# Attention scores as 64-row products, one PSUM bank per head, with q copied once and the second element's means moved

## The chip, the cores and the metric

The kernel runs on one core of a Trainium2 chip. A core has five engines that run their own instruction streams: TensorE (PE: matrix products and, as PEld, the loading of the stationary operand), VectorE (DVE), ScalarE (ACT), GpSimd (POOL) and SyncE (SP), which here issues all transfers between memory and the on-chip buffers. Products land in PSUM, which is used here as eight banks of 128 partitions by 512 float32. The metric is the device time of one execution in microseconds; the time of a kernel is the median of its runs.

## The reference

Attention over 4 elements of a batch, 8 heads, 768 positions and 64 values per head, then a two-layer network over the 3,072 rows. Each position sees its neighbours within 15 positions and a summary of each of the 24 blocks of 32 positions: the maximum of the block's keys and the mean of its values.

```python
block, window = (32, 16)
nb = S // block
scale = 1.0 / np.sqrt(D)
k_sum = k.reshape(B, H, nb, block, D).max(axis=3)
v_sum = v.reshape(B, H, nb, block, D).mean(axis=3)
scores_l = scale * np.matmul(q, k.transpose(0, 1, 3, 2))
mask_l = np.abs(pos[:, None] - pos[None, :]) < window
scores_s = scale * np.einsum('bhsd,bhnd->bhsn', q, k_sum)
scores_s = scores_s + np.log(block)
scores_l_m = np.where(mask_l, scores_l, -1000000000.0)
scores_all = np.concatenate([scores_l_m, scores_s], axis=-1)
...
a = np.exp(scores_all)
a = a / (np.sum(a, axis=-1, keepdims=True) + 1e-09)
v_all = np.concatenate([v, v_sum], axis=2)
return np.matmul(a, v_all).astype(np.float32)
```

```python
h = x @ w_in
g = h - np.tanh(h)
return (g @ w_out).astype(np.float32)
```

`w_in` is 512 x 2048 and `w_out` 2048 x 512. They arrive as 8-byte floats and are turned into float32 on the chip. All arithmetic has float32 accuracy.

## The kernel before

**Units.** Each element is cut into two halves of 384 positions, so there are eight units `u` (`NU`), each of three tiles `i` of 128 positions (`NT`). Heads go in four pairs `p` per unit, so there are 32 pairs (u, p); two pairs share a group `g` of four heads, for which q, k and v are loaded together (`load_qk`, `load_v`).

**One pair.** `prep` transposes q and k of a pair on PE, two heads on top of each other: head `a` = 0 on partitions 0 to 63, head 1 on 64 to 127. The k side is copied whole into `kf`. The q side is copied into `qf` of shape 128 x 2 x 384: head 0 into `[0:64, 0]`, head 1 into `[64:128, 1]`, two copies of 64 partitions ("q high"); the other two quarters were filled with zeros at the start by `zeros`, on POOL. `prep_sums` puts the block maxima into `kf` between the tiles ("top put"). `score` then makes, for each tile, head and half tile of 64 positions, one product of 118 columns: the 128 rows of `qf[:, a]` against 118 columns of `kf`, in which the zeros remove the other head. A pair has twelve such products. They land in two banks: tiles 0 and 1 in the first, tile 2 in the second (`score_of`), the half tiles on output partitions 0 to 63 and 64 to 127. `softmax` takes the minimum with the mask from the bank (DVE, "min"), the exponential (ACT, "exp"), the sum, its inverse and the normalising product; `transpose_probs` turns the probabilities on PE ("p turn"), into the score banks and bank `pX`, and copies them out ("p out"). `value` makes twelve products of 64 columns per pair, and one entry of the plan (`scores_and_values`) issues the values of one pair directly ahead of the scores of the next.

**Block summaries.** For elements 0 and 1 they are made in the head of the kernel. `load_part` loads one piece of k or v (192 KB); `top_pair` makes the maxima of a pair's keys (two "top pre" on DVE, three transposes on PE, a "top max" on DVE), `sum_pair` the means of a pair's values with twelve small products against `blk`, and `place_v` turns the means of two pairs ("mean turn") into `mean`, from where a transfer puts them into `vw` (`put_mean`). `TOPS` and `SUMS` name the slot at which each (element, pair) has its turn; the loads take buffers of the rings `gt`, `gu`, `gv`, `gh`, `gl`, which the network needs only later. In the kernel before, the pieces for element 0 and element 1 both lie in slots 0 to 15. Elements 2 and 3 are handled later in another way (`sum_chunks`, `finish_k`, `finish_v`).

**The network.** `convert` loads one block of weights (512 KB) at a time, 32 in all, and turns it into float32 in four steps on DVE and ACT. Unit 0 uses whole float32 weights (`wf`): for each of 16 blocks `f` an input product ("in", four products of 384 columns, eight instructions, in one of two banks `pH`), the activation on ACT, POOL or DVE, and three output products ("out", 512 columns, in banks `pY0` to `pY2`). For later units the weights are split into two parts of reduced precision, and each product becomes three that run faster. From unit 2 on, half of the input products are replaced by a scheme with seven products for eight, whose operands are stored to and read back from a scratch tensor `scr`.

**The order of the work.** The main loop runs over slots `j`; unit 0 and its attention fill slots 0 to 15, and the network of unit `u` follows its attention by `LAG` = 22 slots. Each piece of work is an entry of a plan with its reads, writes and a cost. `Plan.schedule` places them on the engines by priority, which is the length of the path behind an entry plus the tables `BIAS` and `KB`; `SL` says when an entry may go to its second engine. The instructions are then issued in that order and stay in it. In the first 100 us, gaps on PE are filled with products of `ident` by itself (`keep_warm`), which nobody reads. Every operation is recorded through one helper, so the profile shows line L72 for all of them, and tiles tell them apart: `q` is `qf`, `k` is `kf`, `pS`, `pX`, `pY` and `pH` are banks, `th` holds the maxima.

The second half of `attention_moe_kernel` repeats the program without the shortcut for small activations; it is behind a test and does not run with these inputs.

Of the kernel before, what the change touches and what calls it, by code (L numbers as in the profile page):

```python
# [15 lines left out]
ALU = mybir.AluOpType  # L16
# [8 lines left out]

PLAIN = 3
# [11 lines left out]

PREP = [0, 2, 6, 11]

TOPS = {0: [(0, 0)], 1: [(0, 2)], 3: [(0, 1)], 5: [(0, 3)], 9: [(1, 3)], 11: [(1, 2)], 13: [(1, 0)], 15: [(1, 1)]}
SUMS = {0: [(0, 0)], 1: [(0, 1), (1, 1)], 8: [(0, 2)], 9: [(0, 3)], 10: [(1, 0)], 11: [(1, 2)], 13: [(1, 3)]}

SIGNED = set()
# [60 lines left out]
class Plan:  # L105
# [56 lines left out]
    def schedule(self, idle):  # L162
# [49 lines left out]
        while total:  # L212
# [88 lines left out]
def program(  # L301
# [129 lines left out]
    ident, mask, blk, ga, small = (made[n,] for n in ("ident", "mask", "blk", "ga", "small"))  # L431
# [21 lines left out]
    def make_blk():  # L453

        gpsimd.memset(blk, 1.0 / 32)
        gpsimd.affine_select(blk, blk, [[1, 3], [-32, NBH]], ALU.is_ge, 0.0, base=0, channel_multiplier=3)
        gpsimd.affine_select(blk, blk, [[-1, 3], [32, NBH]], ALU.is_ge, 0.0, base=31, channel_multiplier=-3)
# [4 lines left out]
    do("const", POOL, 0.7, make_blk, w=[BLK])  # L462
# [14 lines left out]
    for j in range(2):  # L477
        buf(("qf", j), f"q{j}", [P, 2, U])
        buf(("kf", j), f"k{j}", [P, KC])
# [5 lines left out]
    rawq, rawk, vw = (made[n,] for n in ("rawq", "rawk", "vw"))  # L485
    RAWQ = [(("rawq",), i) for i in range(NT)]
    RAWK = [(("rawk",), i) for i in range(4)]

    def vw_keys(i, half):
        return [(("vw",), (i, half, n)) for n in range(3)]  # L490

# [5 lines left out]
    for j in range(2):  # L497
        zeros(j)
# [839 lines left out]
```

## Time and profile before

| | us |
|---|---|
| runs | 730.04, 727.91, 725.0 |
| median | 727.91 |
| profiled execution | 722.92 |
| its span, first to last instruction | 721.2 |

The profile is that of one execution, and its times are counted from its first instruction. A row of instructions has the start, the duration, the engine, the line, the operation with output and inputs, and how many of them were merged; the bracket behind it says how long the engine had been idle and for what. In a row of the chain of waits only the start, the length and the work stand. The merged busy time of PE counts pipelined products, so the distance between starts, or the chain, says what a group really takes.

### The profile page before, as it was taken

Reading aid. Unit: us, or ns where it says so; the run is one execution under the profiler, and the core shown is the slowest. Engines: PE = TensorE matmul, PEld = TensorE weight load, DVE = VectorE, ACT = ScalarE, POOL = GpSimd, SP = SyncE. Lnnn points to the kernel's source line nnn. Section 1 sums busy time; section 2 is a strip of 40 time slices with the busy share of each in tenths; the row PEclk is TensorE's granted clock in tenths of the full one; section 3 lists DMA queues with packets and bytes.
Section 4 is the critical chain, followed back from the end, with each engine's and each line's share of the span. In section 5 each row is a group of like instructions: output and inputs, shape, how many; then the busy total and the mean of one; then the engine's idle time right before and its main releaser. Section 6 shows DMA issues by size and latency. Waiting matters only on the chain.

```text
span 721.2 us, 14213 instructions
## 1 busy us (share of the span) xinstructions
PE 688.8 (96%) x4787; PEld 572.6 (79%) x4787; DVE 431.6 (60%) x1180; ACT 482.3 (67%) x1411; POOL 256.4 (36%) x394
## 2 busy tenths in 40 slices
PE   6898799999999998999999999999999999999995
PEld 5685455558888787889988878998998888999884
DVE  4567878986996645654766557554568533444241
ACT  3467577767789776775897577555669965334981
POOL 3011421131246617422457563433345531111440
PEclk9999899999999999999999999999999999999998
DMA  9989968965665677567465557566544323444101
GB/s 211 234 239 239 307 197 225 281 200 151 202 171 166 179 238 206 138 196 190 123 182 170 164 136 225 142 180 177 170 146 147 119 87 115 147 162 145 45 1 50
DMA packets 158002, 122.67 MB, mean 170 GB/s; under 512 B 94816, under 2 KB 123744, under 8 KB 157920
## 3 DMA queue, kind: packets, MB, share of 16 engines
q1 hardware_dynamic: 157920, 121.67, 58.4%
q8 instruction: 40, 0.66, 0.4%
q14 instruction: 42, 0.34, 0.1%
HBM read 96.21 MB, written 23.07 MB: 165 GB/s over the span
## 4 chain that ended last, share of the span: by engine, by line
PE 77%; DMA 9%; ACT 5%; DVE 3%; SPq 3%; POOL 2%; issue 1%; POOLq 0%; ACTq 0%; DVEq 0%
PE pY L72 34%; PE pH L72 31%; PE pS L72 7%; PE pX L72 5%; SPq L72 3%; DMA wraw<-in_moe_w_in_dram 2%; DMA wraw<-scr 1%; POOL gh L72 1%; ACT prob L72 1%; ACT gu L72 1%; DMA wraw<-in_moe_w_out_dram 1%; DMA gh<-in_v_dram 1%; ACT tmp L72 1%; DVE wf L72 1%; DVE tmp L72 1%
## 5 line engine op out<-in xcount | busy, mean ns | idle before, releaser
L72 PE MATMUL pY<-wf,gh 128*128 128x512 f32 x432 | 178.9, 443 | 5.2 <-POOL gh L72 5.2
L72 PE MATMUL pH<-wh,wraw 128*128 128x384 f32 x672 | 175.3, 342 | 1.3 <-DMA wraw<-scr 1.3
L72 PE MATMUL pY<-wh,gh 128*128 128x512 f32 x336 | 139.4, 415 | 0.0
L72 PE MATMUL pY<-wh,gl 128*128 128x512 f32 x336 | 132.8, 395 | 0.0
L72 PEld LDWEIGHTS pH<-wh,wraw 128*128 128x128 f32 x672 | 120.2, 188 | 9.6 <-DMA wraw<-scr 1.5
L72 POOL TENSOR_TENSOR gu<-gu,gt 128x384 f32<-128x384 f32 x59 | 61.4, 1041 | 185.8 <-ACT gu L72 161.5
L72 ACT ACTIVATE prob<-prob,stat 128x118 f32<-128x118 f32 x248 | 92.3, 384 | 21.3 <-DVE stat L72 20.9
L72 PEld LDWEIGHTS pY<-wf,gh 128*128 128x128 f32 x432 | 80.6, 190 | 30.4 <-issue 12.7
L72 PE MATMUL pH<-wf,wraw 128*128 128x384 f32 x309 | 104.1, 337 | 0.0
L72 PEld LDWEIGHTS pY<-wh,gl 128*128 128x128 f32 x336 | 63.2, 188 | 14.8
L72 PEld LDWEIGHTS pY<-wh,gh 128*128 128x128 f32 x336 | 63.4, 189 | 12.1 <-issue 2.3
L72 ACT ACTIVATE gu<-gu 128x384 f32<-128x384 f32 x128 | 66.9, 523 | 2.2
L72 PE MATMUL pH<-o,wf 128*128 128x384 f32 x188 | 65.3, 446 | 1.6 <-DVE wf L72 1.6
L72 PEld LDWEIGHTS pH<-wf,wraw 128*128 128x128 f32 x309 | 58.0, 188 | 0.0
L72 ACT ACTIVATE gh<-gu 128x384 fp32r<-128x384 f32 x67 | 34.8, 522 | 30.9 <-PE pY L72 21.6
L72 DVE COPY gv<-pH 128x384 f32<-128x384 f32 x50 | 27.9, 558 | 42.4 <-PE pH L72 42.4
L72 DVE CUSTOM_DVE_ANT_0 prob<-pS,mask 128x118 f32<-128x118 f32 x180 | 40.7, 273 | 20.7 <-PE pS L72 20.6
L72 PEld LDWEIGHTS pH<-o,wf 128*128 128x128 f32 x188 | 35.7, 193 | 20.5 <-issue 4.4
L72 ACT ACTIVATE gt<-gu 128x384 f32<-128x384 f32 x42 | 21.9, 523 | 37.1 <-DVE gu L72 36.9
L72 DVE TENSOR_TENSOR gl<-gu,gh 128x384 fp32r<-128x384 f32 x38 | 22.7, 596 | 39.6 <-ACT gh L72 35.7
L72 POOL TENSOR_TENSOR gl<-gu,gh 128x384 fp32r<-128x384 f32 x32 | 33.6, 1055 | 29.4 <-ACT gh L72 27.7
L72 POOL TENSOR_TENSOR gh<-gu,gt 128x384 f32<-128x384 f32 x15 | 23.3, 1555 | 57.3 <-ACT gu L72 33.9
(212 smaller groups left out, 1298.2 us busy)
## 6 DMA issues: line engine op xcount, KB each, us to landing
wraw<-scr SPq DMA_DIRECT2D x75, 512.0 KB
wraw<-in_moe_w_in_dram SPq DMA_DIRECT2D x16, 512.0 KB
wraw<-in_moe_w_out_dram SPq DMA_DIRECT2D x16, 512.0 KB
scr<-wraw SPq DMA_DIRECT2D x16, 512.0 KB
rawq<-in_q_dram SPq DMA_DIRECT2D x48, 128.0 KB
out_dram<-tmp SPq DMA_DIRECT2D x24, 256.0 KB
wraw<-scr SPq DMA_DIRECT2D x21, 256.0 KB
rawk<-in_k_dram SPq DMA_DIRECT2D x32, 128.0 KB
```

The costliest lines, as they stand in the source:

```text
L72: return lambda *args, **kwargs: self._tc.keep_in_program_order(op(*args, **kwargs))
```

## The change

The scores: `qf` loses its second half for one of two buffers (128 x 1 x 384; the other keeps its size because later tiles share it), and the zeros are gone. One copy of 128 partitions replaces two of 64. Each score product takes only the 64 rows of its head, from both `qf` and `kf`, and head `a` lands in bank `a` with its three tiles side by side. The order of the products is now tile, half tile, head.

The means: the pieces of element 1 leave `TOPS` and `SUMS`. Its loads are issued in slots 16 (pairs 0 and 1) and 26 (pairs 2 and 3), eight each time, into the buffers `wh22` to `wh29`; sums and maxima follow in slots 22, 23, 28, 29 and 24, 25, 30, 31, in the banks `pH`. A piece of v is now one head with all its positions, six consecutive positions to a partition, in runs of 1,536 bytes where it was a pair's half in runs of 768 bytes. `sum_pair` has twelve products of 24 columns, all six of a head one after the other, where it had twelve of 12 columns with the heads alternating; `blk` has six planes of 24 columns and lies in the buffer `wh30`.

The plan: `BIAS`, `SL` and `KB` have other numbers throughout, some costs are other numbers, and the products of `keep_warm` are planned with a gap of 0.1 us. The functions `in_runs` and `by_runs` and the branches that use them are not taken, since `RUNS` is 0.

```diff
+RUNS = 0
...
-TOPS = {0: [(0, 0)], 1: [(0, 2)], 3: [(0, 1)], 5: [(0, 3)], 9: [(1, 3)], 11: [(1, 2)], 13: [(1, 0)], 15: [(1, 1)]}
-SUMS = {0: [(0, 0)], 1: [(0, 1), (1, 1)], 8: [(0, 2)], 9: [(0, 3)], 10: [(1, 0)], 11: [(1, 2)], 13: [(1, 3)]}
+TOPS = {0: [(0, 0)], 1: [(0, 2)], 3: [(0, 1)], 5: [(0, 3)]}
+SUMS = {0: [(0, 0)], 1: [(0, 1)], 8: [(0, 2)], 9: [(0, 3)]}
...
-                    d.out = free[PE] = clock.run(free[PE], cost)
+                    d.out = clock.run(free[PE], cost)
+                    free[PE] = d.out + 0.1
...
-    fixed(("blk",), [P, 3, NBH])
+    buf(("blk",), f"wh{2 * NF - 2}", [P, 6, NB])
...
-        buf(("qf", j), f"q{j}", [P, 2, U])
+        buf(("qf", j), f"q{j}", [P, 2 if j else 1, U])
...
-    def zeros(j):
-        for a in range(2):
-            o = 64 * (1 - a)
-            do("const", POOL, 0.75, lambda a=a, o=o: gpsimd.memset(at(("qf", j))[o:o + 64, a], 0.0), w=[(("qf", j), "zero%d" % a)])
...
-                sync.dma_start(st.rearrange("r (a t d) -> r a t d", a=2, t=3), v[b, hs, ts].rearrange("a (r t) d -> r a t d", t=3))
+                sync.dma_start(st, v[b, 2 * p + h].rearrange("(r t) d -> r (t d)", t=6))
...
-            for h in range(2):
-                st = at(("v", b, p, h)).rearrange("r (a t d) -> r a t d", a=2, t=3)
-                for t in range(3):
-                    for a in range(2):
-                        tensor.matmul(at(ps)[D * a:D * (a + 1), NBH * h:NBH * (h + 1)], st[:, a, t], blk[:, t], start=t == 0, stop=t == 2)
+            for a in range(2):
+                st = at(("v", b, p, a)).rearrange("r (t d) -> r t d", t=6)
+                for t in range(6):
+                    tensor.matmul(at(ps)[D * a:D * (a + 1), :NB], st[:, t], at(("blk",))[:, t], start=t == 0, stop=t == 5)
...
-        for a in range(2):
-            rows = slice(64 * a, 64 * a + 64)
-            either("q high", {ACT: 0.42, DVE: 0.5}, lambda e, a=a, rows=rows: copy(e, at(qf)[rows, a], at(pq)[rows, :U], -1.0 / math.sqrt(D)), r=[(pq, 0)], w=[(qf, a)])
+
+        either("q high", {ACT: 0.42, DVE: 0.5}, lambda e: copy(e, at(qf)[:, 0], at(pq)[:, :U], -1.0 / math.sqrt(D)), r=[(pq, 0)], w=[(qf, 0)])
...
-    def score_of(u, p, i):
-        return ("s", u, p, i // 2), 2 * N2 * (i % 2)
+    def score_of(u, p, i, a):
+        return ("s", u, p, a), N2 * i
...
-            s, c = score_of(u, p, i)
-            for a in range(2):
-                for half in range(2):
+            for half in range(2):
+                for a in range(2):
+                    s, c = score_of(u, p, i, a)
                     k0 = KS * i + 64 + 64 * half
-                    tensor.matmul(at(s)[64 * half:64 * half + 64, c + N2 * a:c + N2 * (a + 1)], at(qf)[:, a, P * i + 64 * half:P * i + 64 * half + 64], at(kf)[:, k0:k0 + N2], start=True, stop=True)
+                    rows = slice(64 * a, 64 * a + 64)
+                    tensor.matmul(at(s)[64 * half:64 * half + 64, c:c + N2], at(qf)[rows, 0, P * i + 64 * half:P * i + 64 * half + 64], at(kf)[rows, k0:k0 + N2], start=True, stop=True)
...
-        if B > 1 and j in (23, 31):
-            place_v(1, (j - 23) // 8, "pS1")
+        if B > 1 and j in (16, 26):
+            for n, (kind, p1, h) in enumerate((kind, p1, h) for kind in "vk" for p1 in range(2) for h in range(2)):
+                load_part(kind, 1, p1 + (j - 16) // 5, h, f"wh{22 + n}")
+        if B > 1 and 22 <= j < 32 and (j - 22) % 6 < 4:
+            g, n = divmod(j - 22, 6)
+            if n < 2:
+                sum_pair(1, PG * g + n, "pH")
+                if n == 1:
+                    place_v(1, g, "pS1")
+            else:
+                top_pair(1, PG * g + n - 2, "pH")
```

More of the change, by code (lines that the diff above doesn't have):

```diff
@@ L430, in program @@
     fixed(("small",), [P, 1])
-    ident, mask, blk, ga, small = (made[n,] for n in ("ident", "mask", "blk", "ga", "small"))
+    ident, mask, ga, small = (made[n,] for n in ("ident", "mask", "ga", "small"))
     def make_ident():
@@ L487, in program, with in_runs, by_runs @@
     RAWK = [(("rawk",), i) for i in range(4)]
+    def in_runs(u):
+        return u < RUNS
+    def by_runs(x, n):
+        return x.rearrange("p i h d -> p (i h d)").rearrange("p (h t d) -> p h t d", h=HG, t=n)
     def vw_keys(i, half):
         return [(("vw",), (i, half, n)) for n in range(3)]
-    def zeros(j):
-        for a in range(2):
-            o = 64 * (1 - a)
-            do("const", POOL, 0.75, lambda a=a, o=o: gpsimd.memset(at(("qf", j))[o:o + 64, a], 0.0), w=[(("qf", j), "zero%d" % a)])
-    for j in range(2):
-        zeros(j)
-    do("const", DVE, 0.2, lambda: vector.memset(rawk[0:79, 0], 0.0), w=[RAWK[0]])
-    do("const", DVE, 0.2, lambda: vector.memset(rawk[96:P, 3], 0.0), w=[RAWK[3]])
+    do("const", DVE, 0.3, lambda: vector.memset(rawk[0:79, 0], 0.0), w=[RAWK[0]])
+    do("const", DVE, 0.3, lambda: vector.memset(rawk[96:P, 3], 0.0), w=[RAWK[3]])
     do("const", DVE, 0.2, lambda: vector.memset(vw[0:WIN, 0, 0], 0.0), w=[vw_keys(0, 0)[0]])
@@ L657, in top_pair @@
                    r=[(st[a], 0)] if a else (), w=[(st[0], 0)])
-        do("top turn", PE, 0.325, lambda: [tensor.transpose(at(ps)[:, P * c:P * (c + 1)], at(st[0])[:, P * c:P * (c + 1)], ident) for c in range(3)],
+        do("top turn", PE, 0.42, lambda: [tensor.transpose(at(ps)[:, P * c:P * (c + 1)], at(st[0])[:, P * c:P * (c + 1)], ident) for c in range(3)],
            r=[(st[0], 0), IDENT], w=[(ps, 0)])
@@ L686, in go @@
                 tensor.matmul(at(ps)[:NB, P * pr:P * (pr + 1)], at(x)[:, pr], ident, start=True, stop=True)
-        do("mean turn", PE, 0.5, go, r=[(x, pr) for pr in range(PG)] + [IDENT], w=[(ps, 0)])
+        do("mean turn", PE, 0.55, go, r=[(x, pr) for pr in range(PG)] + [IDENT], w=[(ps, 0)])
         do("mean out", ACT, 0.28, lambda: scalar.activation(mean[32 * g:32 * g + NB], at(ps)[:NB, :HG * D], AF.Copy), r=[(ps, 0)], w=[MEAN[g]])
@@ L798, in transposes @@
         def transposes(ps, raw, n):
+            if in_runs(u):
+                for t in range(n):
+                    for a in (1, 0):
+                        c = ((hs.start + a) * n + t - a) * D
+                        tensor.transpose(at(ps)[:D * (a + 1), :P * n].rearrange("p (r t) -> p t r", t=n)[:, t], raw.rearrange("p i h d -> p (i h d)")[:, c:c + D * (a + 1)], ident)
+                return
             for i in range(n):
                 tensor.transpose(at(ps)[:, P * i:P * (i + 1)], raw[:, i, hs].rearrange("p a d -> p (a d)"), ident)
-        do("q turn", PE, 0.285, lambda: transposes(pq, rawq, NT), r=[*RAWQ, IDENT], w=[(pq, 0)])
-        do("k turn", PE, 0.395, lambda: transposes(pk, rawk, 4), r=[*RAWK, IDENT], w=[(pk, 0)])
-        for a in range(2):
-            rows = slice(64 * a, 64 * a + 64)
-            either("q high", {ACT: 0.42, DVE: 0.5}, lambda e, a=a, rows=rows: copy(e, at(qf)[rows, a], at(pq)[rows, :U], -1.0 / math.sqrt(D)), r=[(pq, 0)], w=[(qf, a)])
+        do("q turn", PE, 0.46 if in_runs(u) else 0.285, lambda: transposes(pq, rawq, NT), r=[*RAWQ, IDENT], w=[(pq, 0)])
+        do("k turn", PE, 0.6 if in_runs(u) else 0.395, lambda: transposes(pk, rawk, 4), r=[*RAWK, IDENT], w=[(pk, 0)])
+        either("q high", {ACT: 0.42, DVE: 0.5}, lambda e: copy(e, at(qf)[:, 0], at(pq)[:, :U], -1.0 / math.sqrt(D)), r=[(pq, 0)], w=[(qf, 0)])
         def runs():
@@ L849, in scores_and_values @@
     def scores_and_values(now, before, tags, px_tag):
-        r, w, cost, parts = [], [], 0.25, []
+        r, w, cost, parts = [], [], 0.13, []
         if before is not None:
             px = bank(("px", *before), px_tag)
-            r, w, cost = r + value_keys(*before), w + [(px, i) for i in range(NT)], cost + 0.75
+            r, w, cost = r + value_keys(*before), w + [(px, i) for i in range(NT)], cost + 0.72
             parts.append(lambda: value(*before))
@@ L857, in scores_and_values @@
             banks = [bank(("s", u, p, n), tag) for n, tag in enumerate(tags)]
-            r, w, cost = r + score_keys(u, p), w + [(x, n) for x in banks for n in range(4)], cost + 1.23
+            r, w, cost = r + score_keys(u, p), w + [(x, n) for x in banks for n in range(NT)], cost + 0.6
             parts.append(lambda: score(*now))
@@ L887, in softmax @@
         for i, a in both:
-            s, _ = score_of(u, p, i)
-            do("min", DVE, 0.21, lambda i=i, a=a: first(i, a), r=[(s, 2 * (i % 2) + a), MASK], w=[(("pr", u, p, i), a), (st, 2 * i + a)])
+            s, _ = score_of(u, p, i, a)
+            do("min", DVE, 0.21, lambda i=i, a=a: first(i, a), r=[(s, i), MASK], w=[(("pr", u, p, i), a), (st, 2 * i + a)])
         for i, a in both:
```

43 lines of the change are left out of this document (28 added, 15 removed).

## The prediction

> **What bounds the kernel now.** I read the page first, then busy time by stage, then the chain of waits, then the instructions of one attention pair, then the issues of the DMA queue.
>
> ```profile
> span 721.2 us, 14213 instructions
> ...
> PE 688.8 (96%) x4787; PEld 572.6 (79%) x4787; DVE 431.6 (60%) x1180; ACT 482.3 (67%) x1411; POOL 256.4 (36%) x394
> ...
> PEclk9999899999999999999999999999999999999998
> DMA  9989968965665677567465557566544323444101
> ```
>
> The span is 721.2 us and TensorE (PE) is busy for 96% of it at nearly full clock; DVE and ACT are far from that (60% and 67%). The DMA share is 80 to 100% in the first eight slices and about half afterwards. So the kernel has a head in which transfers matter and a long rest in which PE does. Busy time by stage shows where one passes into the other:
>
> ```profile
> 0.00:52.30 52.30, 42.46 (x557) 37.16 (x558) 29.52 (x114) 23.34 (x85) 9.53 (x40) 1.00 0.89 223
> 52.30:163.80 111.50, 103.64 (x534) 58.45 (x532) 92.99 (x220) 77.86 (x217) 28.25 (x27) 0.97 0.85 242
> 163.80:240.00 76.20, 76.20 (x554) 67.17 (x553) 57.90 (x150) 62.04 (x185) 31.27 (x46) 1.00 0.57 171
> 240.00:300.00 60.00, 54.47 (x446) 46.23 (x445) 35.82 (x113) 45.30 (x144) 30.12 (x49) 1.00 0.68 196
> 300.00:580.00 280.00, 279.07 (x2071) 247.95 (x2070) 166.33 (x500) 200.47 (x606) 124.00 (x203) 1.00 0.57 165
> 580.00:710.00 130.00, 130.00 (x625) 113.60 (x624) 49.08 (x86) 71.47 (x178) 33.23 (x32) 1.00 0.28 94
> ```
>
> (Columns: stretch, length, busy time of PE, weight loads, DVE, ACT, POOL, then clock, DMA share, GB/s.) From 163.8 us to 710 us PE is idle for 6.5 us in 546. There a microsecond of PE work taken away is a microsecond of time. In the second stretch (the MoE of the first half-element, whose weights are converted meanwhile) PE is idle for 7.9 of 111.5 us, DVE is at 83% and DMA at 85%. In the first stretch PE is busy for 42.5 us, but much of it is filler:
>
> ```profile
> L72 PE MATMUL pS<-ident 128*128 128x128 f32 x110 | 16.4, 298 | 0.5 <-DVE q L72 0.3
> ```
>
> These 16.4 us are the warm-up products of `keep_warm`, so PE does some 26 us of work in the first 52.3 us. What the head waits for is seen in the chain of waits and the queue:
>
> ```profile
> by line: PE pH L72 18.5%; PE pY L72 17.8%; DMA wraw<-in_moe_w_in_dram 9.8%; SPq L72 7.2%; PE pS L72 6.4%; POOL gh L72 4.6%; ACT prob L72 3.6%; DMA wraw<-in_moe_w_out_dram 3.5%; DMA gh<-in_v_dram 3.4%; PE pX L72 3.4%; issue 3.2%; DVE tmp L72
> ...
> 27.70 6.06 DMA gh<-in_v_dram
> ...
> 44.97 1.55 SPq L72
> ...
> 47.76 4.91 DMA wraw<-in_moe_w_in_dram
> ```
> ```profile
> 52.31 2.75 PE L72 MATMUL pH<-o,wf 128*128 128x384 f32 x8
> ```
>
> (Chain: start, length, what.) A transfer of v, then issues on the DMA queue (SPq), then a weight transfer lead up to the first MoE product at 52.31 us.
>
> **The change, part by part.** *Scores.* One pair's scores and the value products just before them, in the chain in the PE-bound stretch:
>
> ```profile
> 186.85 0.85 PE pX L72 x24
> 187.70 1.21 PE pS L72 x24
> 188.91 1.58 PE pY L72 x6
> ...
> 196.34 1.39 PE pY L72 x6
> ```
> ```profile
> 102.89 2.58 PE pH L72 x8
> ```
>
> The 12 score products are 24 instructions (each float32 product is two) and take 1.21 us. An undivided float32 product of 384 columns takes 2.58/8 = 0.32 us an instruction, 0.84 ns a column; 118 columns alone would be 0.099 us and 24 of them 2.38 us. The measured 1.21 is half of that: the two halves of output partitions (`half`) already run side by side. The new products use 64 rows as well, and neighbours in the order write to two banks from two halves of the rows. Four at a time would give 0.605 us. The bound from the other side is the pace of small products:
>
> ```profile
> 11.35 0.86 PEld L72 LDWEIGHTS pY<-blk,gu 128*64 128x64 f32 x24
> ```
> ```profile
> 186.78 0.78 PEld L72 LDWEIGHTS pX<-probT,vw 118*64 118x64 f32 x24 [0.37 <-PE pY L72]
> 187.47 1.21 PEld L72 LDWEIGHTS pS<-k,q 128*64 128x64 f32 x24
> ```
>
> 24 products of only 12 columns still need 0.86 us, so something other than columns paces them. The value products (64 columns, 24 instructions) take 187.47 - 186.78 = 0.69 us up to the next group, where their columns alone ask for 0.84 ns x 64 x 12 = 0.645 us: 0.045 us more than columns. New scores therefore lie between 0.605 and 0.86 us. I take 0.605 + 0.045 = 0.65, by the value products, which are nearest in kind: 0.56 us saved a pair, between 0.35 and 0.605.
>
> Against that stands a third change of layout. PE now goes from whole products to half-width ones (values, scores) and back; the first group after the scores costs 1.58 instead of 1.39 us, so 0.19 us is paid for going back. The step from values to scores costs nothing now, since both use 128 x 64; afterwards the scores are 64 x 64. Between 0 (this step now) and 0.19 us a pair, I take the middle, 0.095. The Trainium skill, "TensorEngine Tiling (Array Packing)", Key Properties, speaks against the change here: a change of tiling mode, unlike a change of tile, drains TensorE. The 0.19 us behind the scores agrees with it, but no row here shows the step from 128 x 64 to 64 x 64; by that rule the sum below would have the full 0.19 and be 2.7 us worse, without it 2.7 us better.
>
> So 0.56 - 0.095 = 0.465 us a pair. How many pairs count:
>
> ```profile
> L72 PE MATMUL pS<-k,q 128*64 128x118 f32 x720 | 41.6, 265 | 0.3 <-ACT k L72 0.3
> ...
> L72 PE MATMUL pY<-k,q 128*64 128x118 f32 x48 | 2.8, 265 | 0.0
> ```
> ```profile
> L72 PE MATMUL pS<-k,q 128*64 128x118 f32 x120 | 6.9, 265 | 0.0
> ```
>
> 768/24 = 32 pairs; four lie in the head beside idle PE and count nothing, 5 lie in the second stretch and 23 behind it. 28 x 0.465 = **13.0 us** (28 x 0.16 = 4.5 to 28 x 0.605 = 16.9).
>
> *Bank by head.* Each of the two score banks now holds one head of three tiles. The first one comes free for the probability transposes one or two `min` later, while exp, guard and normal of tile 0 still follow: 0.
>
> *q copied once.*
>
> ```profile
> L72 ACT ACTIVATE q<-pS 64x384 f32<-64x384 f32 x34 | 16.4, 483 | 4.2 <-PE pS L72 2.3 <-DVE q L72 1.4
> ...
> L72 DVE TENSOR_SCALAR q<-pS 64x384 f32<-64x384 f32 x22 | 12.1, 552 | 5.1 <-PE pS L72 4.4 <-ACT q L72 0.3
> ...
> L72 DVE TENSOR_REDUCE th<-pH 128x24 f32<-128x384 f32 x8 | 4.4, 550 | 1.7 <-PE pH L72 1.7
> ...
> L72 DVE TENSOR_TENSOR gt<-gt 128x192 f32<-128x192 f32 x3 | 1.1, 359 | 3.7 <-DMA gt<-in_k_dram 3.7
> ```
>
> 64 copies of half the partitions become 32 of all, at the same columns and so about the same time: 32 x 0.5 = 16 us less on ACT and DVE together, over the whole span. Both have idle time there, and PE covers it: 0 to 3 us, I take **1**. If PE ceased to be the cover, ACT at 67% would be next. The zero fills of q (four on POOL) go, `blk` grows from 36 to 144 elements a partition (POOL too): both lie beside the first transfers, 0. `keep_warm` products are planned 0.1 us apart, so there are fewer of them, beside idle PE; the clock of the first stretch is 1.00, and I count 0 as long as it stays so. The branches under `in_runs` are not taken (`RUNS` is 0).
>
> *Means of the second element moved.* Half of 32 transfers leave the head:
>
> ```profile
> gt<-in_k_dram SPq DMA_DIRECT2D x6, 192.0 KB
> ...
> gt<-in_v_dram SPq DMA_DIRECT2D x1, 192.0 KB
> ```
> ```profile
> 0.79 0.98 SPq L72 DMA_DIRECT2D gt<-in_k_dram  x2
> ...
> 50.04 0.63 SPq L72 DMA_DIRECT2D gv<-in_v_dram  x1
> ```
>
> Ten such groups (first and last shown) make 32 issues of 192 KB between 0.79 and 50.04 us; 16 belong to element 1. They are 3.15 MB: 14.1 us of transfers at the 223 GB/s of the first stretch, and 16 x 0.49 = 7.8 us of SP. Both resources are taken almost without a break there, so the first MoE product comes 7.8 to 14.1 us earlier; nothing earlier is the other bound, if it hangs on the attention chain alone. I take **10**. v in runs of 1,536 instead of 768 bytes is the same bytes; it is in that bound.
>
> What leaves the head comes back in slots 16 to 31, in the second stretch: 16 issues (8 us of SP, 13 us of DMA, whose share there is 0.85 of 111.5 us, 16.7 us free, so it just fits); on PE four `sum` groups and four transposes; on DVE 4 x (2 x 0.36 + 0.55) = 5.1 us, at 83% now. A `sum` group is 0.86 us now; the new one runs six products in a row on one half, between the same 0.86 and twice that, 1.7: I take 1.3. A transpose group of three is some 0.5:
>
> ```profile
> 23.13 0.55 PE L72 MATMUL pH<-ident,gt 128*128 128x128 f32 x3 [0.17 <-DVE gt L72]
> ```
>
> 4 x (1.3 + 0.5) = 7.2 us of PE. PE has 7.9 us idle there and slots 22 to 31 leave room, so I count half, **-3.6** (0 to -7.2). The DVE work waits for nothing on PE's path but `top put` of the third half-element: 0 to -5.1, I take -1, which the single q copy returns.
>
> Sum: 13.0 + 1 + 10 - 3.6 - 1 = 19.4 us. The profiled execution took 722.9 us (span 721.2), so 703.5 for such a one; the three runs shown have a median of 727.9, 5 us above it, and against that I forecast **708**.
>
> The tables that order the work (`BIAS`, `SL`, `KB`) are new throughout, so single waits will move. No row prices that; the 6.5 us of PE's idle time behind 163.8 us could go, and as much could come: 0.
>
> **The rivals.** *A, the halves of rows do not run side by side.* Then a product of 64 rows takes as long as one of 128 and 1.21 us stays, with up to 0.19 for the switch. For it: no row shows 64-row products. Against: column halves do overlap in the chain. Time: 727.9 - (19.4 - 13.0) + 28 x 0.19 (5.3) = 727, from 721 without the switch to 731 with less from the head. That is the case that the change does not do what it says.
>
> *B, the moved means stall the input products.* `sum` and `top` of element 1 now take banks `pH`, which the MoE input products take in turn. An `in` must then wait until DVE or ACT has emptied the bank, its g comes later, and the `out` products, behind it in PE's order, wait for that g. What one late g costs stands in the trace:
>
> ```profile
> 77.86 1.02 PE L72 MATMUL pY<-wf,gh 128*128 128x512 f32 x2
> ...
> 85.45 2.07 PE L72 MATMUL pY<-wf,gh 128*128 128x512 f32 x2 [3.87 <-POOL gh L72]
> ...
> 88.17 3.88 PE L72 MATMUL pH<-o,wf 128*128 128x384 f32 x8
> ```
> ```profile
> 80.00:90.00 10.00, 6.13 (x13) 2.95 (x12) 7.46 (x14) 3.75 (x9) 5.23 (x1) 0.68 0.99 260
> ```
>
> 3.87 us idle, and then the granted clock of 0.68 stretches the next groups (2.07 against 1.02 for two `pY`, 3.88 against the 2.75 of the row at 52.31 for eight `pH`): 6.0 us a stall. With 19.4/6.0, at the fourth of the eight groups, the gain is gone; from the fifth it is slower by over 1%: 708.5 + 30 = 738. Against: emptying takes DVE 0.55 us (`th`), and two `pH` buffers alternate.
>
> *C, all at their good ends*: 16.9 + 14.1 + 1 = 32 us, 696. For it: rows and issues are that dense. Against: the moved work must run somewhere.
>
> **How the numbers follow.** Forecast 0.67 (its own range 698 to 720), A 0.17, B 0.08, C 0.08. About 1% (7.3 us) is what a measurement of this kernel can tell from no change. Faster by over 1% (under 720.6): forecast and C, 0.75; within 1%: A, 0.17; slower: B, 0.08. The range of 696 to 728 leaves out B, half of C and half of A, 0.20.
>
> **What would show it.** Right, if the 24 score instructions of a pair take about 0.65 us in the chain; if the first `pH` product of the MoE starts near 42 us; if the group behind the scores still costs about 0.19 us more than its like; if q copies have 128 partitions and count 32. A is shown by 1.2 us a pair; B by waits of `pH` products for DVE `th` or ACT `sum` and by clock below 0.9 between 50 and 110 us. Wrong besides, if PE idles by more than 20 us behind the first MoE product: then the new order, not the products, sets the time.

## The result and the profile after

The changed kernel takes 708.12 us (median of 4 runs, 707.62 to 709.4); beside it on the same chip the kernel before took 728.97 (4 runs, 725.0 to 733.34). The ratio is 0.9715, with a 95% interval of 0.9656 to 0.9774: faster. The forecast was 708.0 in a range of 696 to 728. The total is right; the sections below show that it is right with other terms than those of the forecast.

A ratio here takes of each kernel only the executions within 1.5% of its fastest on that chip, while a median takes all of them; this matters for the kernel before, whose executions spread from 714 to 735 us over the chips, where the four of the changed kernel lie between 707.6 and 709.4. On the chip of this ratio all four executions of the kernel before took 725 us or more. Three kernels within 2.2 us of the changed one (experiments 3, 5 and 9) ran beside 11 to 25 executions of the kernel before, some of them near 715, and have ratios of 0.9825 to 0.9867. So the gain of some 21 us holds for this chip and by the medians; against the shorter executions of the kernel before it is 10 to 13 us.

The page of the changed kernel, in the profiled execution (708.07 us, span 706.0); kernel lines that read L72 before read L74 now:

```profile
span 706.0 us, 14126 instructions
...
PE 677.9 (96%) x4761; PEld 561.1 (79%) x4761; DVE 413.1 (59%) x1151; ACT 486.5 (69%) x1424; POOL 245.3 (35%) x374
...
PEclk9999999999999999999999999999999999999998
DMA  9789898966565768657665546755545222553101
```

PE is at 96% as before, and its busy time has fallen from 688.8 to 677.9 us: 10.9 of the 15.2 us by which this span is shorter. The chain of waits on this page is empty but for its last instruction, so the rest is read from busy time by stage, cut where the first product of the network (the MoE) starts and where the first product of the next unit starts:

```profile
0.00:48.60 48.60, 40.27 (x480) 34.80 (x481) 24.54 (x108) 25.82 (x92) 5.34 (x26) 0.96 0.80 206
48.60:152.50 103.90, 101.99 (x583) 58.19 (x581) 94.59 (x222) 72.33 (x205) 18.93 (x20) 1.00 0.91 270
152.50:706.00 553.50, 535.65 (x3704) 468.10 (x3702) 293.97 (x822) 388.34 (x1130) 220.98 (x328) 0.99 0.51 153
```
```profile
0.00:52.31 52.31, 42.47 (x557) 37.16 (x558) 29.52 (x114) 23.34 (x85) 9.53 (x40) 1.00 0.89 223
52.31:163.80 111.49, 103.63 (x534) 58.44 (x532) 92.99 (x220) 77.86 (x217) 28.25 (x27) 0.97 0.85 242
163.80:721.00 557.20, 542.66 (x3701) 477.00 (x3699) 309.13 (x846) 381.08 (x1110) 218.62 (x328) 0.99 0.51 151
```

(Stretch, length, busy time of PE, weight loads, DVE, ACT, POOL; then clock, which is the share of full speed that TensorE was granted, DMA share, GB/s; the changed kernel first.) The head is 3.7 us shorter, the second stretch 7.6, the rest 3.7 (553.5 against 557.2). In the second stretch PE idles for 1.9 us where it idled for 7.9, at a clock of 1.00 in place of 0.97, and DMA is busier (0.91 against 0.85) with the moved loads. The stretch that gives most is thus not the long one full of scores, but the one into which work was moved.

One attention pair behind the MoE of the first half-element, from the instructions of the weight load queue:

```profile
187.42 0.78 PEld L74 LDWEIGHTS pX<-probT,vw 118*64 118x64 f32 x24 [0.25 <-issue]
188.27 0.61 PEld L74 LDWEIGHTS pS<-k,q 64*64 64x64 f32 x24
189.03 0.19 PEld L74 LDWEIGHTS pY<-wh,gh 128*128 128x128 f32 x1 [0.15 <-issue]
```

The scores take 0.61 us for 1.21. From the first value product to the next whole product it is 189.03 - 187.42 = 1.61 us; in the kernel before, where the first two rows of the block stand in the forecast and the next is

```profile
188.84 0.19 PEld L72 LDWEIGHTS pY<-wh,gh 128*128 128x128 f32 x1 [0.15 <-issue]
```

it was 188.84 - 186.78 = 2.06 us. So 0.45 us a pair, where the forecast had 0.465.

The head, as PE's and the DMA queue's instructions show it:

```profile
42.32 0.34 PE L74 MATMUL pX<-probT,vw 118*64 118x64 f32 x4 [2.37 <-DMA vw<-mean]
...
48.59 2.75 PE L74 MATMUL pH<-o,wf 128*128 128x384 f32 x8
...
51.59 1.37 PE L74 MATMUL pH<-wh,wh 128*64 128x24 f32 x24
52.89 0.94 PE L74 MATMUL pS<-ident 128*128 128x128 f32 x6
```
```profile
29.80 7.28 SPq L74 DMA_DIRECT2D vw<-in_v_dram  x9
...
38.48 2.17 SPq L74 DMA_DIRECT2D vw<-mean  x2
```

The first MoE product starts at 48.59 us (52.31 before; forecast near 42). PE stands for 2.37 us at the value products of a pair because the means have not landed: `vw<-mean` is issued at 38.48, behind nine loads of `vw` that hold the queue for 7.28 us. Behind this wait the clock is 0.72 from 45 to 50 us, where it was 1.00 in the kernel before. The third row is a moved `sum` group; what follows it starts 1.30 us later.

Copies of q, and PE's waits for the products g that POOL makes (before and after):

```profile
L74 ACT ACTIVATE q<-pS 128x384 f32<-128x384 f32 x20 | 9.7, 487 | 1.4 <-PE pS L74 1.3
...
L74 DVE TENSOR_SCALAR q<-pS 128x384 f32<-128x384 f32 x8 | 4.5, 558 | 6.0 <-PE pS L74 5.8
```
```profile
PE pY L72 <- POOL gh L72: 5.2, 2, 3.9
```
```profile
PE pY L74 <- POOL gh L74: 1.9, 1, 1.9
```

The copies have 128 partitions and the same duration (487 and 558 ns against 483 and 552 for half the partitions): twice the work in the same time. The wait for `gh` (total, times, longest) falls from 5.2 to 1.9 us.

### The profile page after: what moved, and what is told of

Read it like the earlier page. It is cut to its first block, busy times and chain, and to the rows that moved or that the text cites. A ratio compares the mean times of both kernels' runs of the same rounds, so it can differ in the third digit from the quotient of the medians.

```text
span 706.0 us, 14126 instructions
## 1 busy us (share of the span) xinstructions
PE 677.9 (96%) x4761; PEld 561.1 (79%) x4761; DVE 413.1 (59%) x1151; ACT 486.5 (69%) x1424; POOL 245.3 (35%) x374
## 5 line engine op out<-in xcount | busy, mean ns | idle before, releaser
L74 PE MATMUL pY<-wf,gh 128*128 128x512 f32 x432 | 179.0, 440 | 1.9 <-POOL gh L74 1.9
L74 PE MATMUL pH<-wh,wraw 128*128 128x384 f32 x672 | 175.9, 343 | 4.2 <-DMA wraw<-scr 4.0
L74 PE MATMUL pY<-wh,gh 128*128 128x512 f32 (+1 forms) x348 | 140.3, 408 | 0.0
L74 PE MATMUL pY<-wh,gl 128*128 128x512 f32 x336 | 132.6, 395 | 0.0
L74 PEld LDWEIGHTS pH<-wh,wraw 128*128 128x128 f32 x672 | 121.5, 189 | 12.8 <-DMA wraw<-scr 3.8
L74 POOL TENSOR_TENSOR gu<-gu,gt 128x384 f32<-128x384 f32 x58 | 61.6, 1063 | 172.7 <-ACT gu L74 158.5
L74 PE MATMUL pH<-wf,wraw 128*128 128x384 f32 x309 | 104.7, 339 | 0.0
L74 ACT ACTIVATE prob<-prob,stat 128x118 f32<-128x118 f32 x251 | 93.4, 384 | 15.9 <-DVE stat L74 13.6
L74 PEld LDWEIGHTS pY<-wf,gh 128*128 128x128 f32 x432 | 80.1, 189 | 24.8 <-issue 8.9
L74 PEld LDWEIGHTS pY<-wh,gl 128*128 128x128 f32 x336 | 63.1, 188 | 15.3
L74 PEld LDWEIGHTS pY<-wh,gh 128*128 128x128 f32 (+1 forms) x348 | 63.9, 186 | 12.2 <-issue 2.2
L74 ACT ACTIVATE gu<-gu 128x384 f32<-128x384 f32 x128 | 66.6, 523 | 2.1
L74 PE MATMUL pH<-o,wf 128*128 128x384 f32 x188 | 64.4, 440 | 0.0
L74 PEld LDWEIGHTS pH<-wf,wraw 128*128 128x128 f32 x309 | 58.4, 189 | 0.0
L74 ACT ACTIVATE gu<-pH 128x384 f32<-128x384 f32 x64 | 31.3, 489 | 36.6 <-PE pH L74 33.1
L74 DVE CUSTOM_DVE_ANT_0 prob<-pS,mask 128x118 f32<-128x118 f32 x180 | 40.9, 275 | 26.4 <-PE pS L74 25.8
L74 PEld LDWEIGHTS pH<-o,wf 128*128 128x128 f32 x188 | 35.0, 189 | 17.7 <-issue 3.0
L74 DVE TENSOR_TENSOR gl<-gu,gh 128x384 fp32r<-128x384 f32 x41 | 23.7, 579 | 41.6 <-ACT gh L74 40.7
L74 POOL TENSOR_TENSOR gh<-gu,gt 128x384 f32<-128x384 f32 x12 | 16.3, 1359 | 75.8 <-DMA wraw<-in_moe_w_in_dram 24.7
L74 POOL TENSOR_TENSOR gl<-gu,gh 128x384 fp32r<-128x384 f32 x29 | 31.4, 1083 | 22.4 <-ACT gh L74 15.7
L74 ACT ACTIVATE gh<-gu 128x384 fp32r<-128x384 f32 x49 | 25.5, 522 | 18.1 <-PE pY L74 10.9
L74 POOL COPY k<-th 64x72 f32<-64x72 f32 (+1 forms) x41 | 11.5, 281 | 72.7 <-PE pS L74 48.5
```

The source lines that it names most:

```text
L74: return lambda *args, **kwargs: self._tc.keep_in_program_order(op(*args, **kwargs))
```

## The experiments

Each edit is given against the kernel named; the text on record stands before what was measured.

**1. The 64-row products alone, in the order of before (two kernels).** Against the kernel before, with its tables, its two copies of q and its zero fills; one bank per head:

```diff
-    def score_of(u, p, i):
-        return ("s", u, p, i // 2), 2 * N2 * (i % 2)
+    def score_of(u, p, i, a):
+        return ("s", u, p, a), N2 * i
...
-            for a in range(2):
-                for half in range(2):
+            for half in range(2):
+                for a in range(2):
...
-                    tensor.matmul(... at(qf)[:, a, ...], at(kf)[:, k0:k0 + N2], ...)
+                    tensor.matmul(... at(qf)[rows, 0, ...], at(kf)[rows, k0:k0 + N2], ...)
```

> The kernel before with the 64-row products, one bank per head and nothing else: two copies of q, the means and the order of all instructions stay as they were (only the twelve products of a pair and the two banks that the min reads differ). Theory, scores: 0.45 us a pair in 28 pairs beside no idle PE, 12.6 us, so 715 to 717 us against 728 before. Rival, order and means: what the products save comes back as waits of PE, and the gain of the change came from the head and the new tables; then 724 to 729 us.

718.04 us (10 runs, 706.24 to 751.72) against 725.81 for the kernel before (25 runs, 715.28 to 734.57), ratio 0.9955 (0.9904 to 1.0006). That is just above the 715 to 717 of the theory, and the interval includes no change. In this kernel one minimum (pair 6, tile 1, head 1, counted from 0) read its bank after the next transpose of q had written there, so one head of one tile was computed from other numbers. The second kernel puts that minimum ahead and is otherwise the same:

> As e1_rows_alone, but the entry of one min (pair 6, tile 1, head 1) is put ahead of the next pair's q transpose in the order in which entries are issued; in e1 that min read its bank after the transpose had been written there, so one head of one tile came from other numbers. The order on every engine is the same. Theory, scores: 8 to 13 us faster than the kernel before, as wide a spread as before. Rival, order and means: within 3 us of the kernel before.

715.57 us (6 runs, 706.77 to 719.32) against 723.79 (11 runs), ratio 0.9892 (0.9805 to 0.9979). By the medians the products alone give 7.8 and 8.2 us. The spread of 13 us is as notable: the profiled execution of the first kernel took 706.24, less than any of the four of the changed kernel, that of the second 718.74. What sets these apart is in experiment 6.

**2. The changed kernel with 128-row products.** The same order and tables; q in two copies with zeros beside them, 128 rows a product:

```diff
-        either("q high", {ACT: 0.42, DVE: 0.5}, lambda e: copy(e, at(qf)[:, 0], ...))
+        either("q high", {ACT: 0.42, DVE: 0.5}, lambda e: [copy(e, at(qf)[64 * a:64 * a + 64, a], ...) for a in range(2)])
...
-                    tensor.matmul(... at(qf)[rows, 0, ...], at(kf)[rows, k0:k0 + N2], ...)
+                    tensor.matmul(... at(qf)[:, a, ...], at(kf)[:, k0:k0 + N2], ...)
```

> The changed kernel with products of 128 rows again (zeros in q, two copies of 64 partitions, order head then half tile), everything else in the order of the changed kernel. Theory, scores: 12 to 14 us slower than the changed kernel, 720 to 722 us. Rival, order and means: 708 to 712 us.

718.22 us (median of 10; nine lie between 716.32 and 722.11, one took 1,745.6, and why stays open), below the 720 to 722 of the theory; the ratio to the kernel before is 0.9951 (0.9905 to 0.9998). Its pair, in the weight load queue:

```profile
192.66 0.78 PEld L74 LDWEIGHTS pX<-probT,vw 118*64 118x64 f32 x24 [0.25 <-issue]
193.36 1.21 PEld L74 LDWEIGHTS pS<-k,q 128*64 128x64 f32 x24
194.72 0.19 PEld L74 LDWEIGHTS pY<-wh,gh 128*128 128x128 f32 x1 [0.15 <-issue]
```

Block 194.72 - 192.66 = 2.06 us, as in the kernel before. With 28 pairs the products should give 28 x 0.45 = 12.6; against the kernel of experiment 3, which ran on the same chip and differs from it in the rows (with the zeros that full rows need and the order of the two inner loops), they give 718.22 - 709.57 = 8.7 us. Some 4 us of what PE saves in the pairs do not reach the end.

Most of these can be found in the traces. From unit 2 on PE needs operands that are read back from `scr`. Its waits for them (total, times, longest) in this kernel, in that of experiment 3 and in the changed kernel:

```profile
PE pH L74 <- DMA wraw<-scr: 1.3, 1, 1.3
```
```profile
PE pH L74 <- DMA wraw<-scr: 2.8, 2, 2.1
```
```profile
PE pH L74 <- DMA wraw<-scr: 4.0, 3, 2.8
```

The longest of them lies between 245 and 251 us in each, and it is the longer the quicker the scores are: 0.74 us where a pair's scores take 1.36 (experiment 4), 1.29 here with 1.21, and 2.05, 2.77 and 3.46 in the three kernels with 0.61 (experiment 3, the changed kernel, experiment 5). From here to experiment 3 the waits grow by 1.5 us and the busy time of the products with `wraw` from 278.9 to 280.7, together 3.3 of the 4 us. These are single executions, and no run makes the read-back quicker.

**3. The changed kernel with q copied in two halves.**

```diff
-        either("q high", {ACT: 0.42, DVE: 0.5}, lambda e: copy(e, at(qf)[:, 0], ...))
+        either("q high", {ACT: 0.42, DVE: 0.5}, lambda e: [copy(e, at(qf)[64 * a:64 * a + 64, 0], ...) for a in range(2)])
```

> The changed kernel with q copied by two instructions of 64 partitions in place of one of 128. Theory: the copies lie beside PE; at most 1 us slower (708 to 709 us), with 32 more copies of some 0.5 us on ACT and DVE. Rival: ACT and DVE are close to the path in the second stretch, then 2 to 5 us slower.

709.57 us (4 runs, 708.67 to 710.44), 1.4 more than the changed kernel, where at most 1 was expected. The two were timed on different chips and their ratios to the kernel before overlap (0.9761 to 0.989 here), so the 1.4 us agrees with the 1 of the forecast and proves little more.

**4. The order of the twelve products.** The changed kernel with the tile as the innermost loop, so that three products in a row use the same quarter of the array; as many products, of the same sizes:

```diff
-        for i in range(NT):
-            for half in range(2):
-                for a in range(2):
+        for half in range(2):
+            for a in range(2):
+                for i in range(NT):
```

> The changed kernel with the order half tile, head, tile: three products in a row on the same quarter of the array. Theory: four quarters run at once only if neighbours in the order differ, so a pair's scores take between 1.2 and 2.4 us in place of 0.61, and the kernel is 17 to 50 us slower (725 to 758 us). Rival, the array overlaps whatever lies in its queue: no change, 708 us.

723.95 us (10 runs, 722.61 to 725.03; ratio to the kernel before 1.0038, 1.0004 to 1.0072), 14.4 more than experiment 3 (which copies q twice a pair) on the same chip and 15.8 more than the changed kernel, a little less than the 17 expected at least. Its block:

```profile
191.51 0.78 PEld L74 LDWEIGHTS pX<-probT,vw 118*64 118x64 f32 x24 [0.25 <-issue]
192.36 1.36 PEld L74 LDWEIGHTS pS<-k,q 64*64 64x64 f32 x24
193.88 0.19 PEld L74 LDWEIGHTS pY<-wh,gh 128*128 128x128 f32 x1 [0.16 <-issue]
```

1.36 us, more than the 128-row products take (1.21). The gain lies in the neighbourhood: products of different quarters overlap when they follow each other, and much less when three of one quarter stand in a row. Rival A (halves of rows do not run side by side, 1.21 us stays) is refuted in the changed order, and in this one the time is even worse than it said. (Both heads in one bank was not tried.)

**5. The scores ahead of the values.** The changed kernel, with the two parts of a joint group exchanged, to see whether the step between the layouts costs only one way:

```diff
-        do("scores" if now is not None else "values", PE, cost, lambda: [go() for go in parts], r=r, w=w)
+        do("scores" if now is not None else "values", PE, cost, lambda: [go() for go in reversed(parts)], r=r, w=w)
```

> The changed kernel with the scores ahead of the value products in each joint group. Theory (every change of layout drains PE, whichever way it goes): the block of values and scores and the group behind it take as long as now, 1.61 us to the next weight load, and the time is 708 us within 2. Rival (only the step from 64 rows of 118 partitions to 64 of 64 costs): 0.16 us a pair less, 4.5 us over 28 pairs, 703.6 us.

710.31 us (4 runs, 709.14 to 711.65). The block is again 1.61 us (190.12 - 188.51):

```profile
188.51 0.61 PEld L74 LDWEIGHTS pS<-k,q 64*64 64x64 f32 x24 [0.25 <-issue]
189.28 0.78 PEld L74 LDWEIGHTS pX<-probT,vw 118*64 118x64 f32 x24 [0.15 <-issue]
190.12 0.19 PEld L74 LDWEIGHTS pY<-wh,gh 128*128 128x128 f32 x1
```

Between scores and values the queue stands for 0.16 us (188.51 + 0.61 to 189.28) and behind the values for 0.06; in the changed kernel it is 0.07 between values and scores and 0.15 behind the scores. The sum is 0.22 both ways, so the theory holds for the block: the order of the two does not matter there. The whole is 2.2 us longer, 0.3 more than was expected, and this is not in the block. PE's waits for `wraw<-scr` (experiment 2) are 6.0 us in the profiled execution, where the changed kernel has 4.0; that they are the reason was not tried.

**6. The POOL products of the second stretch.** The profiled executions of before's order that are long have two POOL products far above the usual 1.0 to 1.5 us. The kernel before run once more:

> The kernel before, unchanged, to see where its executions differ. Theory, late g: they differ by how long POOL takes for single g products (5.23 and 3.07 us in the execution shown, where most take 1.0 to 1.3) and by the clock behind the idle time of PE; an execution near 715 us has no POOL product over 3 us in the second stretch and a clock of 1.00 there, one near 730 has at least as many as the first. Rival, transfers: POOL looks alike and the first MoE product starts at another time.

732.1 us, and its POOL in the second stretch:

```profile
82.92 5.32 POOL L72 TENSOR_TENSOR gh<-gu,gt 128x384 f32<-128x384 f32 x1 [1.95 <-PE pS L72]
...
147.14 7.68 POOL L72 TENSOR_TENSOR gh<-gu,gt 128x384 f32<-128x384 f32 x2 [8.60 <-ACT gu L72]
```

One product in 5.32 us and two in 7.68. The long execution of experiment 1 (718.74 us) has PE waiting for them as well:

```profile
PE pY L72 <- POOL gh L72: 8.4, 2, 5.0
```

So the next kernel is the kernel before with three of these products (the 4th, 12th and 13th that POOL makes in the first half-element) made by DVE at the same places:

```diff
+    pool_g = 0
...
-            t.go(engines[t.engine])
+            late = False
+            if t.kind == "g" and t.engine == POOL and t.name[1] < 16:
+                pool_g += 1
+                late = pool_g in (4, 12, 13)
+            t.go(vector if late else engines[t.engine])
```

> The kernel before, with three products g of the first half-element (the 4th, 12th and 13th that POOL makes there) made by DVE at the same places of its order; nothing else changed. In the traces of the kernel before these took 5.2 to 6.7 us (the 4th and one of the other two) against 1.0 to 1.5 us for the others, and the output products stood behind them. Theory (these stalls, with the lower clock behind them, are what the order of before loses in the second stretch beyond the means): 5 to 9 us faster than the kernel before on the same chip, a ratio of 0.988 to 0.993, and no wait of PE for gh over 1 us between 76 and 150 us. Rival (the stalls are hidden by what PE is short of later, or another wait takes their place): ratio 0.997 to 1.003, within 2 us.

716.18 us (12 runs, 713.29 to 718.03) against 727.57 for the kernel before on the same chip (17 runs, 715.03 to 732.05): 11.4 us by the medians; the ratio is 0.9947 (0.9916 to 0.9978), 4 us. The theory had 5 to 9 us and 0.988 to 0.993, the rival no more than 2 us: the result lies above the theory by the medians and between the two by the ratio. No wait of PE for a product g of POOL is left, and three moved instructions take away most of the spread. PE in the two places (70 to 95 and 140 to 165 us), first in the repeat of the kernel before, then here:

```profile
70.00:95.00 25.00, 21.64 (x88) 11.67 (x88) 18.81 (x42) 14.24 (x41) 9.09 (x5) 0.93 0.95 285
140.00:165.00 25.00, 20.04 (x101) 10.88 (x101) 15.69 (x44) 12.57 (x36) 7.68 (x2) 0.93 0.65 208
```
```profile
70.00:95.00 25.00, 25.00 (x120) 14.16 (x119) 22.97 (x62) 18.83 (x56) 4.01 (x5) 1.00 0.94 288
140.00:165.00 25.00, 25.00 (x130) 15.04 (x129) 19.40 (x50) 17.62 (x51) 4.44 (x6) 1.00 0.73 219
```

PE's busy time goes from 21.64 and 20.04 of 25 us to 25.00 and 25.00, its clock from 0.93 to 1.00, and the three products take 0.55 to 0.56 us each on DVE. A late g costs twice: PE stands, and then runs at a lower clock. The short execution of experiment 1 (706.24 us: the order of before, with 64-row products) shows the same two places without stalls:

```profile
70.00:95.00 25.00, 24.90 (x119) 13.12 (x118) 23.68 (x61) 20.55 (x61) 7.30 (x8) 1.00 1.02 317
140.00:165.00 25.00, 25.00 (x140) 16.50 (x139) 18.58 (x47) 17.19 (x50) 6.02 (x7) 1.00 0.62 175
```

So where the stalls do not come, the order of before with the new products can be as quick as the changed kernel; this is seen in the shortest execution of each kernel of experiment 1 (706.24 and 706.77), and only the first has a trace. That every long execution of the kernel before has these stalls is likely from the two traces with both (722.92 and 732.1 us) and not shown for each.

**7. Without the tables.** `BIAS`, `SL` and `KB` emptied in both kernels, so that the planner orders the work by its own costs:

```diff
-BIAS = {('const', 0): -137.9, ...
+BIAS = {}
...
-SL = {('g', 0, 'vector'): 0, ...
+SL = {}
...
-KB = {('chunk load', 0): 26.3, ...
+KB = {}
```

> The kernel before with BIAS, SL and KB empty: same work, order by path length alone. Theory: slower than with its tables, 740 to 790 us; with e8 it is the base for what the change does without tables.

> The changed kernel with BIAS, SL and KB empty. Theory, the work sets the gain: 12 to 22 us faster than e7. Rival, the tables set it: within 5 us of e7, since each table was fitted to its own kernel.

777.95 us (4 runs, 773.61 to 778.82) for the kernel before and 760.69 (4 runs, 758.84 to 762.11) for the changed one, both on one chip: 17.3 us remain. So the work can carry a gain of this size without the new tables; what these add in the planned order is another question (experiment 6), and each set is worth some 50 us to its kernel. In the traces of these two kernels and of experiment 8 each of the 16 products g that POOL makes for the first half-element takes 1.00 to 1.54 us, although two of the three have the means in the head. So the long ones seem to belong to the planned order of before and not to the place of the means (one trace of each); the changed kernel still has one (3.23 us at 79.67).

**8. The means put back.** The changed kernel without tables and with the means of the second element in the head again:

```diff
-TOPS = {0: [(0, 0)], 1: [(0, 2)], 3: [(0, 1)], 5: [(0, 3)]}
+TOPS = {0: [(0, 0)], 1: [(0, 2)], 3: [(0, 1)], 5: [(0, 3)], 9: [(1, 3)], 11: [(1, 2)], 13: [(1, 0)], 15: [(1, 1)]}
...
-SUMS = {0: [(0, 0)], 1: [(0, 1)], 8: [(0, 2)], 9: [(0, 3)]}
+SUMS = {0: [(0, 0)], 1: [(0, 1), (1, 1)], 8: [(0, 2)], 9: [(0, 3)], 10: [(1, 0)], 11: [(1, 2)], 13: [(1, 3)]}
...
-        if B > 1 and j in (16, 26):
...
+        if B > 1 and j in (23, 31):
+            place_v(1, (j - 23) // 8, "pS1")
```

> The changed kernel with the three tables of offsets empty, as in the run that took 760.7 us, and with the means of the second element back in the head: their loads, sums, maxima and transposes are issued where the kernel before has them. Theory (the head carries eight to ten microseconds of the change, by the means): 765 to 772 us, between 760.7 and the 778.0 of the kernel before with empty tables, and the first product of the first MoE starts 5 us or more later than the 56.3 us seen there. Rival (the means give nothing, because the head hangs on the attention chain and the moved work costs PE what it saves): 758 to 763 us, first product within 3 us of 56.3.

765.74 us (4 runs, 762.71 to 769.93), 5.1 more than the 760.69 of experiment 7 (on another chip). The first MoE product of the two, with the means moved and with the means back:

```profile
56.29 2.75 PE L74 MATMUL pH<-o,wf 128*128 128x384 f32 x8
```
```profile
72.60 7.91 PE L74 MATMUL pH<-o,wf 128*128 128x384 f32 x24
```

And busy time in the second stretch, up to about the first product of the next unit, in the same order:

```profile
56.30:178.20 121.90, 111.37 (x619) 63.89 (x618) 96.74 (x219) 76.55 (x199) 22.07 (x20) 0.94 0.80 243
```
```profile
72.60:190.60 118.00, 106.46 (x537) 60.37 (x536) 83.08 (x188) 67.63 (x180) 21.03 (x20) 0.93 0.66 203
```

16.3 us later at the start, 3.8 at the end of these two executions (5.1 by the medians). In the second stretch PE has 4.9 us less to do (106.46 against 111.37), which shortens it by 3.9; the rest of the span gives back another 8.6 (764.2 - 190.6 against 760.4 - 178.2). The other 12.2 of the 17.3 us come with the rest of the change (products, copies, costs, `keep_warm`); they were not taken apart without the tables.

**9. Sums with alternating halves.** In the changed kernel a `sum` group runs twelve instructions on one half of the output partitions and then twelve on the other; here they alternate, as before the change:

```diff
-            for a in range(2):
-                st = at(("v", b, p, a)).rearrange("r (t d) -> r t d", t=6)
-                for t in range(6):
+            for t in range(6):
+                for a in range(2):
+                    st = at(("v", b, p, a)).rearrange("r (t d) -> r t d", t=6)
```

> The changed kernel with the products of a sum group in the order of before, alternating between the two halves of output partitions. Theory (neighbours on different quarters of the array run side by side): a group of 24 takes 0.9 us in place of 1.30, four such groups lie in the stretch where PE is nearly always busy, so 1.8 us less, some 706.3 us. Rival (the groups lie beside a wait for weights anyway): 708 us, within 0.5 us of the changed kernel, though a group is shorter.

705.91 us (6 runs, 704.51 to 710.95). The first group:

```profile
52.47 0.89 PE L74 MATMUL pH<-wh,wh 128*64 128x24 f32 x24
```

0.89 for 1.37 us, and 2.2 us less than the changed kernel, where 1.8 were expected. Four of its six runs lie below the lowest of the changed kernel and two (709.35, 710.95) do not; the ratios to the kernel before overlap (0.9761 to 0.99 here). That it is faster than the changed kernel is likely and not shown.

## Why the prediction was right, and where it was not

**Scores, 13.0 us.** The mechanism and its price a pair were right. 0.61 us against the 0.65 taken; the step from the values (118 x 64) to the scores (64 x 64) costs 0.16 us (0.85 from start to start, where it was 0.69) against the 0.095 taken; the net is 0.45 against 0.465. The Trainium skill, "TensorEngine Tiling (Array Packing)", Key Properties, has a change of tiling mode drain TensorE; the 0.16 us shows a cost at a step between two layouts that both fill half the columns, so the full 0.19 would have been the better choice. What failed is that each of the 28 pairs counts in full: the products are worth 8.7 us to the whole (experiments 2 and 3) and 8 in the order of before (experiment 1), against 28 x 0.45 = 12.6. The forecast's sentence on the stretch from 163.8 us, "There a microsecond of PE work taken away is a microsecond of time", was too strong: behind the second stretch PE's idle time rises (553.50 - 535.65 = 17.9 us against 557.20 - 542.66 = 14.5, from the two tables by stage, to the end of the span). What came up there is the read-back from `scr` (experiment 2): its waits were hidden or short as long as PE was slower, and the forecast has no term for them.

**q copied once, 1 us.** Measured 1.4, within what the two chips allow.

**Means moved, 10 - 3.6 - 1 = 5.4 us.** Without the tables they are worth 5.1 us (experiment 8), which is the sum by other terms. With the tables the first term failed: the first MoE product came 3.7 us earlier, not 10. The forecast named the reason as its lower bound ("nothing earlier is the other bound, if it hangs on the attention chain alone"): PE waits there for the means and the values of an attention pair, not for the transfers that were taken away. Two readings of the forecast had pointed the other way. The weight transfer in its chain (47.76 + 4.91 = 52.67 us) ends 0.36 us after the first MoE product has started, so that chain does not lead to this product. And the DMA share is not 80 to 100% in all of the first eight slices: the sixth digit is a 6. The clock of the first stretch, for which the forecast counted 0 as long as it stayed at 1.00, is 0.96; whether the gap in `keep_warm` has a part in that beside the 2.37 us wait was not tried. The moved work was sized well: the first `sum` group takes 1.30 us (1.3 taken), and PE takes the work on with 1.9 us of idle time in the stretch.

**Tables, 0.** This is the missing term. The forecast saw one late g (3.87 us of idle time and a clock of 0.68, 6.0 us in all) and used it only as the price for rival B; it did not ask what the changed kernel would do with that stall itself. The stall belongs to the order of before: three products g moved to DVE there give 11.4 us by the medians and 4 by the ratio. The changed order has one such wait of 1.9 us. The balance closes with it: the kernel before without these stalls takes 716.18, and with 8.7 us for the products that is 707.5; the changed kernel takes 708.12. By the ratios it closes as well: 8.7 and 4 us against the 12.6 that the 0.9825 of experiment 3 stands for. And the changed kernel with 128-row products (718.22, experiment 2) is no quicker than the kernel before without the stalls (716.18). So in the planned order the moved means and the single copy seem to leave next to nothing at the end, beside the products and the missing stalls. This balance takes its figures from several chips, and no run puts the means back under the tables: it is an argument and not shown.

**Rivals.** A: refuted (0.61 us); with the loop over tiles as the inner one it would have been nearly right (1.36 us a pair and 723.95, where it had 1.21 and 727; experiment 4). B: no wait of `pH` for the emptied banks decides anything; the clock in the second stretch is 1.00. C: its good ends were reached for the scores of a pair (0.61 of 0.605), not for the head.

**The signs.** The score instructions (0.61 us for about 0.65) and the copies (20 and 8 in the rows above and 4 from `pH`, so 32) came as forecast, the first MoE product did not (48.59 for 42). PE idles for 1.9 + 17.9 = 19.8 us behind it, just below the 20 that were to show that the new order decides. The kernel before has 22.4 by the same count, so this sign could not tell the two apart.

So the forecast hit 708 in part by luck: two terms too large (4.3 of the scores, some 5 of the means) stood against one that was left out (the stalls). The median of 727.9 was the right base for this chip; the profiled execution of 722.9 lies nearer the lower group of the kernel's executions.

## What to carry to other kernels

When products fill half the rows or half the columns of the array, order them so that neighbours lie in different quarters: the same twelve products took 0.61 us one way and 1.36 the other. When a trace of the present kernel shows a stall of several microseconds that hangs on the order, give its end a term and a chance of its own before a change that replans the order, and look at the spread of the runs: 20 us between executions is a hint that something in the order lies on an edge. A saving on the engine that is busy for 96% still reached the end at only 8.7 of 12.6 us: look for the transfers that this engine will meet earlier.

## What was not expected of the hardware

A product of 128 x 384 elements on POOL takes 1.0 to 1.5 us as a rule, and in single places of the same program 5.23 us (from 80 to 90 us of the kernel before, DVE busy for 7.46 of the 10) or 7.68 for two. DVE converts weights beside it in these places. Where the product that took 5.23 us took 1.00 (the 706.24 us execution of experiment 1, at 80.10), a DVE operation beside it took 1.09 us in place of 0.68, as if one of the two had to wait for the other; that this is the cause was not tried. The same product on DVE took 0.55 us there, and PE, kept supplied, held a clock of 1.00 where it had been 0.93. Three products in a row on one quarter of the array are slower (1.36 us for twelve) than the same ones over the whole height of rows (1.21).
